# Weight decoding beside a fused attention and MLP: low parts on GpSimd, and fewer decoding steps among the early pairs

## The chip, the cores and the metric

One NeuronCore of one Trainium2 chip runs the whole program. The metric is device microseconds (us) of one execution. Five engines work beside each other, each taking its own instructions strictly in the order of its row: TensorE (PE, with its weight loads as PEld), VectorE (DVE), ScalarE (ACT), GpSimd (POOL) and SyncE (SP, which issues the transfers). [...]

## The reference

```python
def reference(q, k, v, n_global, n_local, moe_w_in, moe_w_out):   # shortened
    scores = q @ k.T / sqrt(64) - slope_h * dist      # 4 batches, 8 heads, 768 tokens, head size 64
    scores = where(is_global | is_local, scores, -1e9)   # 8 global keys, 96 local ones
    a = exp(scores - max); a = a / (sum(a) + 1e-9)
    x = (a @ v).transpose(0, 2, 1, 3).reshape(3072, 512)
    h = x @ w_in                                     # 512 x 2048
    g = h * clip(h + 3, 0, 6) / 6
    return g @ w_out                                 # 2048 x 512
```

The weights arrive as 64-bit floats. Before they can be used, each must be decoded into a high part and a low part of reduced precision, whose sum carries nearly the full 32 bits. A product of two such pairs takes three matmuls (high by high, low by high, high by low).

## The kernel before, in words

**Tiles.** The 3072 tokens are eight blocks of 384. A block has four pairs of heads (pair `n`, `n` from 0 to 31), and an MLP of sixteen slices `f` of 128 hidden units. Slice `f` takes `first` (12 matmuls, x by `w1`, into a bank `hp`), then the gate (ACT relu L185 and DVE L186 write `g`), `high` (`gh`, the rounded `g`), `rest` (`gl` = `g` - `gh`, L199), and `second` (9 matmuls with `w2` into `acc`, started by `finish`). `finish` of one slice stands on PE behind `first` of the next slice. `g` has one buffer, so the next relu waits until `gl` has been made.

**Decoding.** The weights come in 32 chunks: chunk 2f is the `w1` part of slice `f`, chunk 2f+1 its `w2` part. `decode` is a generator with four steps to a chunk: L444 and L445 on DVE clear and shift the word `wz`; the low part of the chunk *before* is made (L450); L453 puts sign and exponent in; L457 adds the last places `we`, ACT takes the magnitude of the next chunk (L410), rounds this one to its high part (L461) and makes the next `we` (L422; for the first six chunks GpSimd makes it, L415). `wz` and `we` have two buffers each; the buffer of `wz` comes free when the low part has been made, so L410 of chunk c+2 waits for the low part of chunk c.

**What sets the order.** The code is one list of instructions. `in_order` pins PE, SP and GpSimd to the order in which the code issues them. DVE and ACT are ordered by a scheduler. Decoding steps are put between the other work by a budget: `work(pe, dve)` adds to the PE time and the DVE time given out, and while the DVE sum is smaller, a decoding step is issued, whose yield is added to it. The DVE sum starts at `LEAD`. `decoded_to(i)` issues whatever is still missing of chunk `i` just before it is used: `halves` calls it for chunk 2f ahead of `first`, and `finish` for chunk 2f+1 ahead of `second`.

**Stages.** Early stage: pairs 0 to 8 are pipelined over three iterations (scores and weighing L891/L895, normalization on GpSimd L915, turning by PE transposes L923/L925, `values` L971, then `put_x` L160/L161); in the last three iterations the first three slices of block 0 stand between the turns. Common stage: 21 steps, whose block (0 or 1) is a digit of `ORDER`; the zeros are slices 3 to 15 of block 0, the ones slices 0 to 7 of block 1. Step s has `first` of its slice, the gate, and then `finish` of step s-1. After it the decoding is over; the rest of block 1 and blocks 2 to 7 follow with the remaining pairs between them.

## Time and profile before

| | |
|---|---|
| median of 3 runs | 655.08 us (653.16 to 655.09) |
| profiled execution | 654.68 us, span on the core 652.9 us |
| PE busy | 639.4 us, 98% of the span |
| DVE busy | 356.9 us, 55% |
| ACT busy | 257.4 us, 39% |
| POOL busy | 167.6 us, 26% |
| TensorE clock granted | 1.0 throughout |

The page has a line for each engine, the span in 40 slices, the DMA queues, the chain that ended last, and the costliest groups of instructions. Views of the trace give the same by window, by group (mean ns of one, and what ended the idle time before), by wait, and row by row (start us, duration us, engine, line, operation, output and inputs). A row that starts before the row above it has ended is pipelined behind it.

### The profile page before, as it was taken

What the parts mean: (1) busy time and instruction counts of PE and PEld (TensorE: products, weight loads), DVE (VectorE), ACT (ScalarE), POOL (GpSimd) and SP (SyncE); (2) the same over time, 40 slices, a digit from 0 to 9 for tenths busy, and PEclk for the clock granted to TensorE, in tenths of its full rate; (3) what the DMA queues carried; (4) which work ended last, traced back from release to release, by engine and by line L of the source; (5) the groups of instructions that cost most, each with busy time, mean ns of one, the idle gap of its engine ahead of it and who ended that gap; (6) DMA issues with size and microseconds to landing.
All of it is one profiled execution on the core that took longest, in us unless ns stands there. A gap on an engine that the chain in (4) does not pass through costs nothing.

```text
span 652.9 us, 13102 instructions
## 1 busy us (share of the span) xinstructions
PE 639.4 (98%) x4761; PEld 564.1 (86%) x4761; DVE 356.9 (55%) x1066; ACT 257.4 (39%) x706; POOL 167.6 (26%) x372
## 2 busy tenths in 40 slices
PE   8989999999999999999999999999999999999997
PEld 7778999997888889988898888888898888989985
DVE  5889999995644554255444454345542554422222
ACT  6897777775423222242313232132222423121111
POOL 5667000001422322034122332123220341202100
PEclk9999999999999999999999999999999999999999
DMA  7675644443565564346553455525643454310001
GB/s 281 182 238 194 189 157 149 143 129 113 126 189 169 147 192 125 90 118 165 164 134 102 117 154 163 141 78 154 184 126 89 122 136 122 94 43 8 1 0 54
DMA packets 47122, 86.23 MB, mean 132 GB/s; under 512 B 6504, under 2 KB 28872, under 8 KB 47048
## 3 DMA queue, kind: packets, MB, share of 16 engines
q1 hardware_dynamic: 46760, 85.03, 44.4%
q8 instruction: 40, 0.66, 0.4%
q14 instruction: 34, 0.28, 0.1%
q10 hardware_dynamic: 288, 0.26, 0.1%
HBM read 60.30 MB, written 24.97 MB: 131 GB/s over the span
## 4 chain that ended last, share of the span: by engine, by line
PE 83%; DVE 6%; ACT 4%; DMA 2%; POOL 2%; issue 2%; SPq 1%; POOLq 0%; ACTq 0%
PE hp L174 38%; PE acc L206 35%; ACT n L895 3%; PE xp L971 3%; PE sp L862 2%; PE sp L971 2%; DMA there<-blocks 1%; POOL n L915 1%; SPq L953 1%; DVE n L891 1%; PE xp L206 1%; PE tp L206 1%; PE sp L206 1%; DVE blocks L937 1%; DVE wz L453 1%
## 5 line engine op out<-in xcount | busy, mean ns | idle before, releaser
L185 ACT ACTIVATE g<-hp,small 128x384 f32<-128x384 f32 x127 | 73.6, 580 | 277.6 <-PE hp L174 173.4
L174 PE MATMUL hp<-xh,w1h 128*128 128x384 f32 x512 | 173.8, 340 | 0.5 <-ACT w1h L461 0.5
L174 PE MATMUL hp<-xh,w1l 128*128 128x384 f32 x512 | 172.3, 337 | 0.5 <-DVE w1l L450 0.5
L174 PE MATMUL hp<-xl,w1h 128*128 128x384 f32 x512 | 171.7, 335 | 0.0
L192 POOL TENSOR_SCALAR gh<-g 128x384 fp32r<-128x384 f32 x104 | 53.6, 515 | 343.6 <-DVE g L186 320.7
L186 DVE SCALAR_TENSOR_TENSOR g<-g,hp 128x384 f32<-128x384 f32 x128 | 70.7, 553 | 123.3 <-ACT g L185 122.1
L206 PE MATMUL acc<-w2h,gh 128*128 128x512 f32 x336 | 133.2, 396 | 0.0
L206 PE MATMUL acc<-w2h,gl 128*128 128x512 f32 x336 | 131.7, 392 | 0.0
L206 PE MATMUL acc<-w2l,gh 128*128 128x512 f32 x336 | 131.6, 392 | 0.0
L199 DVE TENSOR_TENSOR gl<-g,gh 128x384 fp32r<-128x384 f32 x128 | 71.5, 559 | 70.7 <-POOL gh L192 58.3
L895 ACT ACTIVATE n<-n,least 128x136 f32<-128x136 f32 (+2 forms) x192 | 79.5, 415 | 65.5 <-DVE least L891 64.8
L174 PEld LDWEIGHTS hp<-xh,w1h 128*128 128x128 f32 x512 | 96.1, 188 | 6.5 <-issue 3.1
L174 PEld LDWEIGHTS hp<-xl,w1h 128*128 128x128 f32 x512 | 96.2, 188 | 2.5
L174 PEld LDWEIGHTS hp<-xh,w1l 128*128 128x128 f32 x512 | 96.1, 188 | 1.1 <-DVE w1l L450 0.8
L915 POOL TENSOR_SCALAR n<-n,sums 128x136 f32<-128x136 f32 (+2 forms) x186 | 81.8, 457 | 38.3 <-DVE sums L906 23.1
L206 PEld LDWEIGHTS acc<-w2h,gh 128*128 128x128 f32 x336 | 63.1, 188 | 15.2 <-issue 3.3
L206 PEld LDWEIGHTS acc<-w2h,gl 128*128 128x128 f32 x336 | 63.1, 188 | 13.7 <-DVE gl L199 0.3
L206 PEld LDWEIGHTS acc<-w2l,gh 128*128 128x128 f32 x336 | 63.1, 188 | 11.4
L937 DVE STREAM_TRANSPOSE blocks<-n 128x256 f32<-128x256 f32 x138 | 51.1, 423 | 25.3 <-POOL n L915 20.8
L895 ACT ACTIVATION_READ_ACCUMULATOR n<-n,least 128x1 f32 x192 | 35.9, 187 | 0.0
L891 DVE CUSTOM_DVE_ANT_0 n<-sp,dl 128x136 f32<-128x136 f32 x60 | 17.7, 295 | 14.7 <-PE tp L862 14.7
L410 ACT ACTIVATE wz<-wst 128x512 f32<-128x512 f32 x32 | 21.5, 674 | 5.7 <-DVE w2l L450 2.8
(119 smaller groups left out, 644.6 us busy)
## 6 DMA issues: line engine op xcount, KB each, us to landing
there<-blocks SPq DMA_DIRECT2D x92, 192.0 KB
wst<-w SPq DMA_DIRECT2D x32, 512.0 KB
weights<-there SPq DMA_DIRECT2D x161, 96.0 KB
load<-pairs SPq DMA_DIRECT2D x31, 444.0 KB
load<-pairs SPq DMA_DIRECT2D x32, 384.0 KB
out<-o SPq DMA_DIRECT2D x23, 256.0 KB
weights<-there SPq DMA_DIRECT2D x23, 24.0 KB
there<-blocks SPq DMA_DIRECT2D x4, 72.0 KB
```

What stands on the lines that cost most here:

```text
L174: self.nc.tensor.matmul(hp, lhsT=self.w1(w, f)[:, kt, :], rhs=a[:, kt, :], start=(n == 0), stop=(n == 3 * NKT - 1))
L185: nc.scalar.activation(out=g, in_=hp, func=AF.Relu, bias=self.three, scale=1.0)
L186: nc.vector.scalar_tensor_tensor(out=g, in0=g, scalar=6.0, in1=hp, op0=ALU.min, op1=ALU.mult)
L192: self.nc.gpsimd.tensor_scalar(out=gh, in0=g, scalar1=1.0, scalar2=0.0, op0=ALU.mult, op1=ALU.add)
L199: self.nc.vector.tensor_tensor(out=gl, in0=g, in1=gh.bitcast(F32), op=ALU.subtract)
L206: self.nc.tensor.matmul(acc[tt], lhsT=a[:, tk], rhs=self.w2(w, f), start=(f == 0 and j == 0), stop=(f == NF - 1 and j == 2))
L410: self.nc.scalar.activation(out=self.z[i].bitcast(F32), in_=words[:, :, 1].bitcast(F32), func=AF.Abs)
L891: nc.vector.tensor_tensor_reduce(out=e[:, j, lo:end], in0=sp[j][:, lo:end], in1=d, op0=ALU.add, op1=ALU.min, scale=scale, scalar=3.0e38, a ...
L895: nc.scalar.activation(out=e[:, j, lo:end], in_=e[:, j, lo:end], func=AF.Exp, bias=self.least[:, i:i + 1], scale=-1.0, accum_out=self.sums ...
L915: nc.gpsimd.tensor_scalar(out=e[:, j, lo:end], in0=e[:, j, lo:end], scalar1=over, scalar2=0.0, op0=ALU.mult, op1=ALU.add)
L937: nc.vector.transpose(out=self.blocks[:, :, s, t].rearrange("p b j q -> p j b q"), in_=e[:, :, c:c + P].rearrange("p j (b q) -> p j b q", ...
L971: nc.tensor.matmul(xps[j * D:(j + 1) * D, t * P:(t + 1) * P], lhsT=vt[0:K, t, j * D:(j + 1) * D], rhs=self.part(t, j, c, K), start=(c == 0 ...
```

## The change

Two constants and two engine assignments change. `LEAD` goes from 6 to 14, so that the DVE budget begins higher and decoding steps come later among the early pairs. `QUIET` = 6 is new: the low part of chunk c is made by GpSimd instead of DVE for c from 6 on, and that decoding step then yields 0 to the budget. In the common stage `halves` gets `low=True`: `gl` is made by GpSimd, and the gate's second share of the DVE budget is 0 instead of 0.47. The new line numbers are one or two higher.

```diff
-LEAD = 6
+LEAD = 14
...
+QUIET = 6
...
-    def rest(self, g, gh):
+    def rest(self, g, gh, pool=False):
         gl = self.lp.tile([P, TB], F32R, name="gl")
-        self.nc.vector.tensor_tensor(out=gl, in0=g, in1=gh.bitcast(F32), op=ALU.subtract)
+        (self.nc.gpsimd if pool else self.nc.vector).tensor_tensor(out=gl, in0=g, in1=gh.bitcast(F32), op=ALU.subtract)
...
-                tt(out=lo, in0=sh(self.z.pop(i - 1).bitcast(F32)), in1=hi.bitcast(F32), op=ALU.subtract)
-            yield 0.6 * b
+                (nc.gpsimd if i > QUIET else nc.vector).tensor_tensor(out=lo, in0=sh(self.z.pop(i - 1).bitcast(F32)),
+                                                                      in1=hi.bitcast(F32), op=ALU.subtract)
+            yield 0.6 * b * (i <= QUIET)
...
-    def halves(self, steps, pool=False):
+    def halves(self, steps, pool=False, low=False):
...
-            gl = self.rest(g, gh)
-            self.work(0, 0.47)
+            gl = self.rest(g, gh, low)
+            self.work(0, 0 if low else 0.47)
...
-            for _ in self.halves(todo):
+            for _ in self.halves(todo, low=True):
```

PE has the same order before and after. Three places show what moves.

GpSimd at the start of the common stage, before: behind the masks (`dl`) stands nothing until the decoding is over, when `blocks` is cleared and the next stage's first query is scaled.

```order
L298 TENSOR_SCALAR dl_1028<-d0_85 32x128
L298 TENSOR_SCALAR dl_1028<-d1_86 32x136
L306 MEMSET blocks_1976 128x3x192
L848 TENSOR_SCALAR load0_72<-load0_72,over_1029 128x384
L192 TENSOR_SCALAR gh_2010<-g_2007 128x384
```

GpSimd at the same place, after (`gl_1056` is the gate of step 0, `gl_1109` of step 1, `gl_1138` of step 2 and so on; the low parts are those of chunks 6, then 7 and 8, 9 and 10, 11, 12).

```order
L299 TENSOR_SCALAR dl_1016<-d1_86 32x136
L200 TENSOR_TENSOR gl_1056<-g_1051,gh_1054 128x384
L451 TENSOR_TENSOR w1l0_145<-wz_1060,w1h0_144 128x4x128
L200 TENSOR_TENSOR gl_1109<-g_1104,gh_1107 128x384
L200 TENSOR_TENSOR gl_1138<-g_1133,gh_1136 128x384
L451 TENSOR_TENSOR w2l0_147<-wz_1081,w2h0_146 128x512
L451 TENSOR_TENSOR w1l0_145<-wz_1142,w1h0_144 128x4x128
L200 TENSOR_TENSOR gl_1191<-g_1186,gh_1189 128x384
L451 TENSOR_TENSOR w2l0_147<-wz_1163,w2h0_146 128x512
L451 TENSOR_TENSOR w1l0_145<-wz_1204,w1h0_144 128x4x128
L200 TENSOR_TENSOR gl_1244<-g_1239,gh_1242 128x384
L451 TENSOR_TENSOR w2l0_147<-wz_1216,w2h0_146 128x512
```

The low part of chunk 7, which `finish` of step 1 reads, now stands behind `gl` of step 2, and those of chunks 9 and 10 behind `gl` of step 3. From step 7 to step 14 two low parts stand behind each `gl`; behind the last low part, that of chunk 31, stand five `gl` alone.

DVE behind the last weighing of the early pairs, before (`wz_813` is chunk 2, `wz_848` chunk 3; chunks 0 and 1 are ready):

```order
L927 COPY pt_744<-hp_743 128x512
L905 TENSOR_SCALAR sums_706<-sums_706 128x6
L906 RECIPROCAL sums_706<-sums_706 128x6
L161 TENSOR_TENSOR xl_154<-xp_750,xh_153 128x384
L457 ISA wz_813<-wz_813,we_814 128x1024
L444 TENSOR_SCALAR wz_848<-wz_848 128x512
L445 TENSOR_SCALAR wz_848<-wz_848 128x512
L450 TENSOR_TENSOR w1l0_145<-wz_813,w1h0_144 128x4x128
L453 SCALAR_TENSOR_TENSOR wz_848<-wst_721,wz_848 128x512
L186 SCALAR_TENSOR_TENSOR g_809<-g_809,hp_796 128x384
```

DVE at the same place, after (`wz_775` and `wz_785` are chunks 0 and 1, `wz_853` is chunk 2, `wz_865` chunk 3):

```order
L929 COPY pt_724<-hp_723 128x512
L459 ISA wz_775<-wz_775,we_776 128x1024
L459 ISA wz_785<-wz_785,we_786 128x1024
L907 TENSOR_SCALAR sums_691<-sums_691 128x6
L908 RECIPROCAL sums_691<-sums_691 128x6
L451 TENSOR_TENSOR w1l0_145<-wz_775,w1h0_144 128x4x128
L162 TENSOR_TENSOR xl_154<-xp_730,xh_153 128x384
L451 TENSOR_TENSOR w2l0_147<-wz_785,w2h0_146 128x512
L187 SCALAR_TENSOR_TENSOR g_808<-g_808,hp_795 128x384
L445 TENSOR_SCALAR wz_853<-wz_853 128x512
L446 TENSOR_SCALAR wz_853<-wz_853 128x512
L200 TENSOR_TENSOR gl_849<-g_808,gh_847 128x384
```

The end of chunks 0 and 1 and all of chunk 2 have moved from among the pairs to behind them. On ACT, the magnitude of chunk 2 now stands behind the relu of the first gate, while before it stood among the early weighing:

```order
L186 ACTIVATE g_808<-hp_795,small_70 128x384
L411 ACTIVATE wz_853<-wst_779 128x512
L929 COPY pt_812<-tp_811 128x512
L195 CAST gh_847<-g_808 128x384
L411 ACTIVATE wz_865<-wst_790 128x512
```

Before, the relu of the first gate had the magnitude of chunk 3 ahead of it, that of chunk 4 behind it:

```order
L410 ACTIVATE wz_848<-wst_721 128x512
L461 CAST w1h0_144<-wz_813 128x4x128
L185 ACTIVATE g_809<-hp_796,small_70 128x384
L927 COPY pt_824<-tp_823 128x512
L410 ACTIVATE wz_911<-wst_818 128x512
```

## Prediction

> **What bounds the kernel now.** I read the engine line of the page first, then the windows, to see where PE is not busy.
>
> ```profile
> PE 639.4 (98%) x4761; PEld 564.1 (86%) x4761; DVE 356.9 (55%) x1066; ACT 257.4 (39%) x706; POOL 167.6 (26%) x372
> ```
>
> ```profile
> core 0: us, PE busy (x) PEld busy (x) DVE busy (x) ACT busy (x) POOL busy (x), PEclk, DMA share, GB/s
> 20.00:40.00 20.00, 17.88 (x191) 14.18 (x187) 17.51 (x74) 17.99 (x65) 13.10 (x27) 1.00 0.70 216
> 40.00:60.00 20.00, 17.57 (x162) 15.50 (x161) 18.64 (x51) 16.93 (x46) 15.19 (x32) 1.00 0.62 203
> 120.00:140.00 20.00, 20.00 (x101) 18.03 (x101) 18.98 (x39) 15.32 (x27) 0.00 (x0) 1.00 0.50 157
> 140.00:160.00 20.00, 19.04 (x137) 16.36 (x137) 14.28 (x32) 11.80 (x22) 2.65 (x4) 1.00 0.27 75
> ```
>
> In the common stage (60 to 150 us) PE is busy all of the time although DVE is at 95%: DVE is full, but nobody waits for it. GpSimd does nothing there. What could be won on PE is in the early stage (2.1 and 2.4 us idle in the two windows) and at the end of the decoding (1.0 us). The waits of PE and its rows say which:
>
> ```profile
> PE tp L923 <- ACT pt L927: 1.0, 1, 1.0
> PE hp L174 <- DVE w1l L450: 0.5, 1, 0.5
> PE hp L174 <- ACT w1h L461: 0.5, 1, 0.5
> ```
>
> ```profile
> 28.44 1.32 PE L971 MATMUL xp<-pt,load 128*64 128x128 f32 x20 [0.55 <-DVE xl L161]
> 32.98 1.32 PE L971 MATMUL xp<-pt,load 128*64 128x128 f32 x20 [0.24 <-DVE xl L161]
> 38.53 1.54 PE L971 MATMUL xp<-pt,load 128*64 128x128 f32 x24 [1.05 <-DVE xl L161]
> 44.31 1.54 PE L971 MATMUL xp<-pt,load 128*64 128x128 f32 x24 [1.42 <-issue]
> 46.63 0.42 PE L174 MATMUL hp<-xh,w1h 128*128 128x384 f32 x1
> 51.21 0.43 PE L174 MATMUL hp<-xh,w1h 128*128 128x384 f32 x1
> ```
>
> Successive `values` rows are one iteration of the pairs. Without decoding on DVE one takes 4.54 us (28.44 to 32.98), with it 5.55 and 5.78. The last two rows are `first` of slices 0 and 1. In the chain, the last `values` of the early stage and what follows:
>
> ```profile
> 63.58 1.25 PE xp L971 x20
> 64.82 2.28 PE hp L174 x12
> 73.34 2.10 PE hp L174 x12
> 75.45 2.08 PE acc L206 x9
> ```
>
> A common step takes PE 2.10 + 2.08 = 4.18 us. The prices of single instructions, from the groups by form:
>
> ```profile
> L185 ACT ACTIVATE g<-hp,small 128x384 f32<-128x384 f32 x127 | 73.6, 580 | 277.6 <-PE hp L174 173.4 <-DVE gl L199 96.3 <-DVE blocks L937 3.2
> L199 DVE TENSOR_TENSOR gl<-g,gh 128x384 fp32r<-128x384 f32 x128 | 71.5, 559 | 70.7 <-POOL gh L192 58.3 <-PE acc L206 12.1 <-POOL load L848 0.3
> L186 DVE SCALAR_TENSOR_TENSOR g<-g,hp 128x384 f32<-128x384 f32 x128 | 70.7, 553 | 123.3 <-ACT g L185 122.1
> L192 POOL TENSOR_SCALAR gh<-g 128x384 fp32r<-128x384 f32 x104 | 53.6, 515 | 343.6 <-DVE g L186 320.7 <-PE acc L206 16.5 <-ACT xh L160 4.0
> L457 DVE CUSTOM_DVE_ANT_0 wz<-wz,we 128x1024 uint16<-128x1024 uint16 x32 | 22.7, 710 | 1.6 <-POOL we L415 0.9
> L453 DVE SCALAR_TENSOR_TENSOR wz<-wst,wz 128x512 int32<-128x512 int32 x32 | 22.5, 704 | 0.0
> L410 ACT ACTIVATE wz<-wst 128x512 f32<-128x512 f32 x32 | 21.5, 674 | 5.7 <-DVE w2l L450 2.8 <-DVE w1l L450 2.3
> L422 ACT ACTIVATE we<-wst 128x512 int32<-128x512 uint32 x26 | 17.5, 674 | 0.0
> L445 DVE TENSOR_SCALAR wz<-wz 128x512 int32<-128x512 int32 x32 | 13.8, 432 | 0.3
> L444 DVE TENSOR_SCALAR wz<-wz 128x512 f32<-128x512 f32 x32 | 13.7, 429 | 0.2 <-ACT wz L410 0.2
> L194 ACT CAST gh<-g 128x384 fp32r<-128x384 f32 x24 | 12.3, 511 | 3.3 <-DVE g L186 2.9
> L450 DVE TENSOR_TENSOR w1l<-wz,w1h 128x512 fp32r<-128x512 f32 x16 | 11.1, 694 | 0.0
> L461 ACT CAST w1h<-wz 128x512 fp32r<-128x512 f32 x16 | 9.9, 621 | 1.7 <-DVE wz L457 1.0
> ```
>
> **The price of the new GpSimd instructions.** No row has a two-input operation of this size there. One-input rows, and DVE beside GpSimd:
>
> ```profile
> 30.78 0.69 POOL L415 TENSOR_SCALAR we<-wst 128x512 int32<-128x512 uint32 x1
> 44.50 2.64 POOL L915 TENSOR_SCALAR n<-n,sums 128x232 f32<-128x232 f32 x6 [3.21 <-DVE least L891]
> 47.22 1.93 POOL L415 TENSOR_SCALAR we<-wst 128x512 int32<-128x512 uint32 x2
> ```
>
> ```profile
> 54.26 1.14 DVE L453 SCALAR_TENSOR_TENSOR wz<-wst,wz 128x512 int32<-128x512 int32 x1
> 55.93 1.15 DVE L457 CUSTOM_DVE_ANT_0 wz<-wz,we 128x1024 uint16<-128x1024 uint16 x1
> ```
>
> Lower ends: what one input costs there, 0.69 us for 128x512 and 0.52 for 128x384. Upper ends: twice that, if the inputs are read one after the other, 1.38 and 1.04. On DVE the second input makes 0.69 (L450) of 0.43 (L444), a factor of 1.6; I take the same here: 1.10 for a low part, 0.83 for `gl`. [...] No run so far shows such an instruction.
>
> **What is taken off DVE** is worth nothing by itself: 26 low parts (18.0 us) and 21 `gl` (11.7 us) lie in a stage where PE waited only at its end. Its last 1.0 us, the two waits of 0.5, goes: -1.0, or 0 if the decoding is late again.
>
> **What costs nothing.** On SP three loads of chunks move behind loads of pairs; the transfers' share of 0.62 in the window from 40 leaves room, and each chunk is loaded two chunks ahead. On GpSimd `blocks` and the next stage's first query now stand behind the last `gl`, some 3.7 us behind the stage's last `first` (2.5 and the two rows' 0.58 and 0.59). Before, the query was scaled at 151.55 and first used in a matmul near 158:
>
> ```profile
> 150.87 0.58 POOL L306 MEMSET blocks<- 128x576 f32 x1 [88.63 <-DVE wz L453]
> 151.55 0.59 POOL L848 TENSOR_SCALAR load<-load,over 128x384 f32<-128x384 f32 x1
> ```
>
> ```profile
> 158.40 1.01 PE acc L862 x47
> ```
>
> So over 2 us of cover stay; if it went, the cost would be what of the 3.7 us stands out, under 2.
>
> **Less decoding among the pairs (term A).** Out of DVE's row between the pairs go two L457, two L450, and L444, L445, L453 of chunk 2: 1.42 + 1.39 + 1.57 = 4.4 us. Two iterations fall from 5.55 and 5.78 to about 4.55 and 4.6, so the pairs are 2.2 us early: the `values` at 44.31 comes at 42.1. But all that work now stands between PE and its first slices. Pair 7 is normalized by 44.2 (2.64 us), then GpSimd makes two `we` (0.69 each, 45.6), DVE two L457 (0.6 more behind the second: 46.4), the sums of pair 8 (0.3) and `w1l` of chunk 0 (0.7, 47.5). The third matmul of `first` 0 needs that, and ten of its twelve follow in 1.8: it ends at 49.3, before at 48.8. Chunk 2 starts behind this gate's relu: relu 0.58, magnitude 0.67, L444 0.43, L445 0.43, `gl` 0.56, L453 0.70, chunk 3's L444 0.43, an `xl` of about `gl`'s size 0.56, L457 0.71, chunk 3's L445 and L453 1.13 (which cover the 0.62 of the high part), `w1l` 0.69. That is 6.9, and 6.4 with overlaps of some 0.05 to 0.08 between neighbours: 55.7. `first` 1 ends at 57.6; it began at 51.21 before and ended near 53.4. PE then has 9.0 us to the last `values` (three turns, `values`, two `second`, `first` 2): 66.6, say 66.7, against 63.58, where before lost 1.0 behind ACT (the wait for `pt` above) that falls away. A = +3.1. It is +1 if chunk 3 and `xl` don't stand in the way, and +5 if two DVE rows stretch as those at 54.26 and 55.93 did, and the `we` as at 47.22.
>
> **GpSimd's fixed row (term B).** A low part waits for the `gl` ahead of it, this one for a gate, that for `first`: relu, L186, L194, `gl`, 0.58 + 0.55 + 0.51 + 0.83 = 2.5 us behind the end of `first`. Between `first` of step s and that of s+1 PE has 2.08 us of work; the first use of a `w1` low part is the third matmul (0.35 us in), that of a `w2` low part the second (0.23 us). Step 0 starts at 67.9 (66.7 and `values` 1.25).
> - Chunk 6 (behind `gl` of step 0, used by `first` of step 1): `first` ends 70.0, `g` 71.35, `gh` behind an L422 72.3, `gl` 73.15, low part 74.25; PE is there at 72.4. +1.85.
> - Chunk 7 (behind `gl` of step 2, used by `finish` of step 1, right behind `first` of step 2): `first` ends 80.4, `g` 81.75, `gh` 82.3, `gl` 83.15, low part 84.25; PE is there at 80.65. +3.6.
> - Chunk 10. The buffers of chunks 9 and 10 come free with the low parts of 7 and 8, at 84.25 and 85.35. From 85.4 on: magnitude 86.05, then DVE with both chunks' rows in turn to 88.5, `we` 88.75, L457 89.5, high part 90.1, next `we` 90.7, and only then the relu of step 3 on ACT, 91.2; gate and `gl` 93.2, low parts 94.3 and 95.4. PE wants it at 90.65. +4.75.
> - Chunk 11 by the same chain behind `gl` of step 4: 103.25 against 101.75, +1.5. Chunk 12 behind `gl` of step 5: 107.6 against 105.45, +2.15.
>
> B = 13.85. With the lower prices the five are 1.15, 2.9, 3.65, 1.15 and 1.35, 10.2 in all; the upper ones give about 16.5. The waits of ACT's L410 for L450 in its group row (2.8 and 2.3) show that the two buffers of `wz` do hold it up.
>
> **The dense steps (term C).** From step 9 to 14 two chunks are decoded per step, in two buffers; each goes round once per step: 0.67 + 0.43 + 0.43 + 0.70 + 0.71 + 0.62 + 1.10 = 4.66, with seven hand-overs of some 0.03 (L415 ends at 31.47, L457 starts at 31.50) 4.9, and 5.0 with something of a gate on DVE between. PE needs 4.18: +0.8 for six steps, C = +4.9. The lower price gives +1.8, the upper one +7.
>
> **Sum**, against the profiled execution: 654.68 + 3.1 + 13.85 + 4.9 - 1.0 = 675.5 us. That execution lies inside the three timed runs, 0.06% under their median, 655.08. From the lower ends it is 654.68 + 1 + 10.2 + 1.8 - 1 = 666.7, from the upper 654.68 + 5 + 16.5 + 7 = 683.2.
>
> **Rivals.**
> *PE stays the bound.* Were the low part of chunk 7 done within 0.23 us of the end of `first` of step 2, GpSimd's row would cost nothing; the pairs' gain of 2.2 and the waits of 1.0 and 1.0 would come through, 654.68 - 4.2 = 650.5, or 653 with half of it. For it speaks that GpSimd is idle in the whole stage; against it that the gate's four instructions alone take 2.5 us, and that the order of that row is fixed. 0.09. Something between that and no change: 0.04.
> *Only the first two waits.* PE, once late, might find the later low parts ready: 654.68 + 3.1 + 1.85 + 3.6 - 1.0 = 662.2. Against it: the buffers tie chunks 9 and 10 to the late low parts, so lateness is passed on. 0.12.
> *DVE stretched beside GpSimd.* L453 and L457 took 1.14 and 1.15 beside L415, 0.44 more than their means. If both do so for both chunks of the six dense steps, 4 x 0.44 x 6 = 10.6 more: 686. For it: those two rows. Against it: most low parts come while DVE waits. 0.07. [...]
>
> **Chances.** Forecast 0.68, first two waits 0.12, stretched 0.07, faster 0.09, between 0.04. The range 661 to 687 takes in the first three but for a little at its ends. About 0.3% (2 us, the spread of the three runs) is what a measurement can tell from no change: faster 0.09, same 0.04, slower 0.87.
>
> **What the profile after would show.** PE's list of waits led by GpSimd's low parts: L451 ahead of L175 and L207, single waits of 3 us and more, all before 115 us; PE well under 20 in the windows from 60 to 120; GpSimd busy 45 us (26 x 1.10 + 21 x 0.83) between 65 and 170; the `values` now at 44.31 about 2 us earlier, `first` 1 some 4 us later; common steps of about 5 us between steps 9 and 14, then 4.18 again. I am wrong if PE is busy throughout the common stage: then either a low part is much shorter than 0.69 or the row is not kept as written. If single waits are there but the later ones are missing, the second rival holds.

## The result, and the profile after

The kernel after takes 707.31 us (median of 4 runs, 704.65 to 707.71), the kernel before 654.88 (653.16 to 655.09): a ratio of 1.0798, 95% interval 1.0766 to 1.0831. The direction was forecast, the size was not: 675.5 us, at most 687. Four executions that ran far longer than the others of their kernel (702 to 2245 us) are left out of all comparisons, which leaves two for the kernel with a third buffer, below, and no interval.

The engine line of the page, and PE's list of waits (engine, line, what it waited for: us in all, times, longest):

```profile
PE 656.9 (93%) x4761; PEld 574.3 (82%) x4761; DVE 358.8 (51%) x1019; ACT 258.7 (37%) x706; POOL 224.0 (32%) x419
```

```profile
PE acc L207 <- POOL gl L200: 9.5, 4, 2.7
PE hp L175 <- POOL w1l L451: 9.2, 4, 3.0
PE sp L207 <- POOL gl L200: 6.3, 3, 2.9
PE acc L207 <- POOL w2l L451: 4.3, 2, 3.9
```

DVE's busy time is larger than before (358.8 against 356.9), although 47 of its instructions, 29.7 us, have gone to GpSimd. The groups by form say where it went:

```profile
L455 DVE SCALAR_TENSOR_TENSOR wz<-wst,wz 128x512 int32<-128x512 int32 x32 | 34.2, 1067 | 0.8
L459 DVE CUSTOM_DVE_ANT_0 wz<-wz,we 128x1024 uint16<-128x1024 uint16 x32 | 29.9, 933 | 3.3 <-POOL we L416 1.3 <-ACT we L423 0.6
L200 POOL TENSOR_TENSOR gl<-g,gh 128x384 fp32r<-128x384 f32 x21 | 24.4, 1160 | 52.0 <-issue 31.0 <-ACT gh L195 17.7 <-PE xp L207 3.2
L451 POOL TENSOR_TENSOR w1l<-wz,w1h 128x512 fp32r<-128x512 f32 x13 | 17.7, 1359 | 15.6 <-ACT w1h L463 15.6
L445 DVE TENSOR_SCALAR wz<-wz 128x512 f32<-128x512 f32 x32 | 15.3, 478 | 20.7 <-ACT wz L411 20.7
```

L455 and L459 (L453 and L457 before) do what they did, in 1067 and 933 ns in place of 704 and 710: 18.8 us more for 32 chunks. And DVE stood idle 20.7 us ahead of L445, waiting for the next magnitude (L411), which itself waited 17.2 us for low parts of GpSimd to give up a `wz`. The windows (columns as before: PE, PEld, DVE, ACT, POOL busy, granted clock) show two different stretches. First one of the kernel before, then the kernel after:

```profile
80.00:100.00 20.00, 20.00 (x103) 18.24 (x102) 19.26 (x40) 15.56 (x28) 0.00 (x0) 1.00 0.49 148
```

```profile
80.00:100.00 20.00, 13.75 (x53) 11.48 (x52) 7.08 (x13) 8.71 (x15) 7.29 (x7) 0.83 0.25 79
100.00:120.00 20.00, 16.03 (x62) 14.11 (x63) 12.81 (x22) 10.27 (x19) 7.05 (x7) 0.83 0.33 104
140.00:160.00 20.00, 15.39 (x62) 12.70 (x60) 19.09 (x26) 12.18 (x21) 9.96 (x7) 0.86 0.46 137
160.00:180.00 20.00, 12.60 (x50) 9.98 (x50) 19.21 (x24) 12.22 (x22) 11.28 (x9) 0.90 0.38 127
```

From 80 to 100 PE, DVE, ACT and GpSimd all wait: PE is busy 13.75 us in place of 20.00, DVE only 7.08 in place of 19.26. From 140 to 180 DVE is full and PE waits for it.

To see where the time is lost I take the relu of a common step's gate as a clock: step 0, 9, 16 and 20 (of 0 to 20). In the kernel before the fourth of these rows starts at 152.26 us and the first three are

```profile
67.14 0.58 ACT L185 ACTIVATE g<-hp,small 128x384 f32<-128x384 f32 x1 [0.24 <-PE hp L174]
104.70 0.58 ACT L185 ACTIVATE g<-hp,small 128x384 f32<-128x384 f32 x1 [1.16 <-PE hp L174]
...
133.96 0.58 ACT L185 ACTIVATE g<-hp,small 128x384 f32<-128x384 f32 x1 [0.94 <-DVE wz L457]
```

In the kernel after the fourth starts at 202.32 us and the first three are

```profile
72.95 0.58 ACT L186 ACTIVATE g<-hp,small 128x384 f32<-128x384 f32 x1 [0.99 <-PE hp L175]
132.04 0.58 ACT L186 ACTIVATE g<-hp,small 128x384 f32<-128x384 f32 x1 [1.46 <-PE hp L175]
...
186.76 0.58 ACT L186 ACTIVATE g<-hp,small 128x384 f32<-128x384 f32 x1
```

The lateness is 5.8, 27.3, 52.8 and 50.1 us: 5.8 before step 0 (term A: 3.1 forecast), 21.5 up to step 9 (term B: 13.85), 25.5 from step 9 to 16 (term C: 4.9), and 2.7 won back at the end of the decoding (1.0 forecast). The end of the span is 50.0 us late too (702.9 against 652.9), so nothing is lost or won behind the decoding. (The profiled executions are 50.0 us apart, the medians 52.4.)

### The profile page after: what moved, and what is told of

Read it like the earlier page. It is cut to its first block, busy times and chain, and to the rows that moved or that the text cites. A ratio compares the mean times of both kernels' runs of the same rounds, so it can differ in the third digit from the quotient of the medians.

```text
span 702.9 us, 13105 instructions
## 1 busy us (share of the span) xinstructions
PE 656.9 (93%) x4761; PEld 574.3 (82%) x4761; DVE 358.8 (51%) x1019; ACT 258.7 (37%) x706; POOL 224.0 (32%) x419
## 4 chain that ended last, share of the span: by engine, by line
PE 68%; DVE 7%; POOL 2%; DMA 2%; issue 2%; ACT 1%; SPq 1%; DVEq 0%; POOLq 0%; ACTq 0%
PE hp L175 31%; PE acc L207 30%; DVE wz L455 2%; PE sp L864 2%; PE xp L973 2%; PE sp L973 2%; DVE wz L459 2%; DMA there<-blocks 1%; SPq L955 1%; DVE wz L446 1%; POOL w2l L451 1%; DVE wz L445 1%; ACT n L897 1%; DVE blocks L939 1%; POOL w1l L451 1%
## 5 line engine op out<-in xcount | busy, mean ns | idle before, releaser
L175 PE MATMUL hp<-xh,w1l 128*128 128x384 f32 x512 | 175.7, 343 | 10.5 <-POOL w1l L451 9.2
L175 PE MATMUL hp<-xh,w1h 128*128 128x384 f32 x512 | 177.1, 346 | 4.2 <-ACT w1h L463 4.2
L175 PE MATMUL hp<-xl,w1h 128*128 128x384 f32 x512 | 174.7, 341 | 0.0
L187 DVE SCALAR_TENSOR_TENSOR g<-g,hp 128x384 f32<-128x384 f32 x128 | 70.7, 552 | 146.2 <-ACT g L186 145.2
L207 PE MATMUL acc<-w2h,gl 128*128 128x512 f32 x336 | 134.4, 400 | 9.5 <-POOL gl L200 9.5
L175 PEld LDWEIGHTS hp<-xh,w1l 128*128 128x128 f32 x512 | 98.6, 192 | 12.4 <-POOL w1l L451 10.5
L175 PEld LDWEIGHTS hp<-xh,w1h 128*128 128x128 f32 x512 | 98.8, 193 | 10.9 <-ACT w1h L463 5.1
L200 DVE TENSOR_TENSOR gl<-g,gh 128x384 fp32r<-128x384 f32 x107 | 59.7, 558 | 70.2 <-POOL gh L193 58.2
L917 POOL TENSOR_SCALAR n<-n,sums 128x136 f32<-128x136 f32 (+2 forms) x186 | 79.2, 444 | 39.6 <-DVE sums L908 25.5
L200 POOL TENSOR_TENSOR gl<-g,gh 128x384 fp32r<-128x384 f32 x21 | 24.4, 1160 | 52.0 <-issue 31.0
L455 DVE SCALAR_TENSOR_TENSOR wz<-wst,wz 128x512 int32<-128x512 int32 x32 | 34.2, 1067 | 0.8
```

The source lines that it names most:

```text
L175: self.nc.tensor.matmul(hp, lhsT=self.w1(w, f)[:, kt, :], rhs=a[:, kt, :], start=(n == 0), stop=(n == 3 * NKT - 1))
L187: nc.vector.scalar_tensor_tensor(out=g, in0=g, scalar=6.0, in1=hp, op0=ALU.min, op1=ALU.mult)
L200: (self.nc.gpsimd if pool else self.nc.vector).tensor_tensor(out=gl, in0=g, in1=gh.bitcast(F32), op=ALU.subtract)
L207: self.nc.tensor.matmul(acc[tt], lhsT=a[:, tk], rhs=self.w2(w, f), start=(f == 0 and j == 0), stop=(f == NF - 1 and j == 2))
L455: stt(out=z, in0=self.raw[i].rearrange("p (c w) -> p c w", w=2)[:, :, 1], scalar=-0x40000000, in1=z, op0=ALU.bitwise_and, op1=ALU.bitwise_or)
L917: nc.gpsimd.tensor_scalar(out=e[:, j, lo:end], in0=e[:, j, lo:end], scalar1=over, scalar2=0.0, op0=ALU.mult, op1=ALU.add)
```

## Experiments

Differences are to the kernel before on the same chip in the same comparison; the last three columns are the lateness gained in the three parts of the trace, read from the relu rows as above. What is gained or won back behind step 16 is not in them.

| kernel | us | against before | ratio (95%) | to step 0 | 0 to 9 | 9 to 16 |
|---|---|---|---|---|---|---|
| after | 707.3 | +52.4 | 1.0798 (1.0766 to 1.0831) | 5.8 | 21.5 | 25.5 |
| LEAD 14 alone | 663.0 | +7.7 | 1.0121 (1.0103 to 1.0139) | 6.9 | 1.2 | 0.8 |
| after, all on DVE again | 662.5 | +7.3 | 1.0113 (1.0091 to 1.0135) | 5.9 | 1.3 | 0.8 |
| `gl` alone | 660.0 | +4.8 | 1.0073 (1.0054 to 1.0093) | -0.1 | 4.2 | 2.7 |
| low parts alone | 679.4 | +24.1 | 1.0378 (1.0351 to 1.0404) | 2.2 | 13.9 | 10.6 |
| both, LEAD and budget of before | 698.1 | +43.2 | 1.0659 (1.0631 to 1.0688) | 1.1 | 21.0 | 9.7 |
| after, LEAD 6 | 694.5 | +39.6 | 1.0599 (1.0572 to 1.0625) | 0.7 | 23.0 | 16.6 |
| after, row not fixed | 685.6 | +30.7 | 1.0468 (1.0440 to 1.0496) | 7.2 | 13.2 | 8.6 |
| same, LEAD 6 | 681.7 | +26.8 | 1.0413 (1.0389 to 1.0438) | 2.2 | 13.5 | 10.3 |
| low parts in quarters | 676.4 | +21.5 | 1.0318 (1.0289 to 1.0346) | 2.4 | 8.5 | 7.3 |
| same, third `wz` | 684.9 | +29.6 | 1.0461 (1.0422 to 1.0500) | 1.8 | 18.8 | 8.3 |
| low parts of one input | 661.5 | +6.2 | 1.0097 (1.0065 to 1.0128) | 1.4 | 3.9 | 2.8 |
| after, all of one input | 680.6 | +25.8 | 1.0403 (1.0373 to 1.0433) | 5.4 | 12.9 | 5.6 |
| after, idle matmuls in waits | 705.9 | +50.6 | 1.0758 (1.0713 to 1.0802) | 7.7 | 21.0 | 24.7 |
| after, third `wz` | 703.3, 705.6 | +48, +50 | none | 5.6 | 22.2 | 20.2 |
| LEAD 9 alone | 660.6 | +5.7 | 1.0087 (1.0072 to 1.0102) | 3.6 | 1.2 | 0.7 |
| last three low parts | 655.3 | +0.4 | 1.0017 (0.9998 to 1.0035) | 0.5 | 0.0 | 0.0 |

### Which part costs what

**LEAD alone.** `-LEAD = 6` / `+LEAD = 14` in the kernel before.

> The kernel before with LEAD at 14 and nothing else: only less of the decoding among the early pairs; all low parts and gl stay on VectorE. My theory (the lateness of the stage's start is a cost by itself, 5.7 us in the trace after: `values` 8 at 69.3 against 63.6): 654.9 + 4 to 6 = 659 to 661, and part of it may grow, since VectorE is full up to the end of the decoding and has 4.4 us more to do there: up to 665. Rival (the lateness comes only with GpSimd's row, or is made good by the common stage's slack): 654 to 656.

662.96: 7.7 more, above my 4 to 6 but inside what I allowed for DVE. PE's rows that waited, around slices 0 and 1 of this kernel:

```profile
48.12 0.69 PE L174 MATMUL hp<-xh,w1l 128*128 128x384 f32 x1 [0.84 <-DVE w1l L450]
57.18 0.46 PE L174 MATMUL hp<-xh,w1h 128*128 128x384 f32 x1 [1.84 <-ACT w1h L461]
```

Slice 1 starts 6 us later than before (51.21), as slice 0's weights are late and chunk 2 stands behind its gate. The lateness is made here (6.9 us at step 0) and is not won back (8.1 at step 20).

**The close packing without GpSimd.** The kernel after, with L451 and L200 given back to `nc.vector`; LEAD and the yields stay.

> The kernel after with its LEAD and its budgets (the decoding as closely packed as there), but the low parts and gl made by VectorE again. My theory (the cost is what GpSimd's instructions do, as waits in its fixed row and as stretching of VectorE, and the clock that follows): most of the 52.4 us go, 660 to 670, what is left being the later start and a VectorE that is late in the close steps. Rival (the close packing of the decoding makes the long steps, whoever does the low parts): 690 to 707, with steps of 7 us and more between 140 and 180.

662.53, as LEAD alone. But the close packing did not stay. DVE's rows show it, when the last instruction of each chunk (L459 in the kernel after, L458 here) is counted between the gates: from step 9 to step 16 the kernel after finishes two chunks in every step, 14 in all, this kernel and the kernel before nine. In every step of the stage this kernel finishes as many as LEAD alone. So the changed budget costs nothing while the work stays on DVE, and 45 of the 52 us come only when the 47 instructions go to GpSimd; whether by what they do or by the closer row on DVE that the scheduler then makes, this run can't say.

**`gl` alone**, and **low parts alone**, each in the kernel before with its LEAD and its budget:

```diff
...
-            for _ in self.halves(todo):            # gl alone
+            for _ in self.halves(todo, low=True):
...
-                tt(out=lo, ...)                    # low parts alone
+                (nc.gpsimd if i > QUIET else nc.vector).tensor_tensor(out=lo, ...)
```

> The kernel before with only the common slices' gl on GpSimd; low parts on VectorE, budgets and LEAD as before. My theory (the waits come from low parts that stand behind a gl in GpSimd's row; gl alone has a whole step until it is used): PE waits for a gl seldom, VectorE is relieved by 0.56 us a step but stretched by some 0.5 us while a gl runs: 653 to 659. Rival (every instruction on GpSimd beside VectorE costs by stretching): 21 x 0.5 to 1.0 us = 10 to 20 more, 665 to 675.

> The kernel before with only the low parts from the seventh chunk on on GpSimd; gl on VectorE, budgets and LEAD as before. My theory of the fixed row (a low part waits because a gl stands ahead of it): these waits go, since nothing stands in GpSimd's row but low parts; what stays is 0.67 us more per chunk in the round of the two wz buffers (some 4.9 us for two chunks against 5.2 that they come apart), and stretched L453 and L457: 656 to 668. Rival (the stretching alone makes the long steps: about 1.6 us for each of 26 chunks on a VectorE that is full): 680 to 700.

`gl` alone came out between the two, near mine. The low parts alone decided against me: 679.4, where the fixed row should have cost nothing, since no `gl` stands in it. PE now waits for the gates that DVE makes (14.7 us), not for a low part: every step from 0 to 16 takes 4.6 to 6.8 us in place of 4.2. The groups of this kernel, and four rows of GpSimd and DVE in order of time:

```profile
L455 DVE SCALAR_TENSOR_TENSOR wz<-wst,wz 128x512 int32<-128x512 int32 x32 | 39.8, 1245 | 0.9
L446 DVE TENSOR_SCALAR wz<-wz 128x512 int32<-128x512 int32 x32 | 22.1, 692 | 0.7
```

```profile
103.21 1.28 POOL L451 TENSOR_TENSOR w1l<-wz,w1h 128x512 fp32r<-128x512 f32 x1 [2.36 <-ACT w1h L463]
103.31 1.73 DVE L455 SCALAR_TENSOR_TENSOR wz<-wst,wz 128x512 int32<-128x512 int32 x1
...
106.60 1.30 POOL L451 TENSOR_TENSOR w2l<-wz,w2h 128x512 fp32r<-128x512 f32 x1 [2.11 <-ACT w2h L463]
106.70 1.48 DVE L446 TENSOR_SCALAR wz<-wz 128x512 int32<-128x512 int32 x1
```

GpSimd begins at 103.21 and ends at 104.49; DVE's L455 begins 0.10 behind it and ends at 105.04, 0.55 behind its end. The row reads as if it stood still until GpSimd is through, and then took most of its usual 0.70. L446, with one input, the same (ends 0.28 behind). It is so each time: between 64 and 190 us, 17 of L455 and 8 of L446 start behind a low part in this way, and all of them end 0.54 to 0.56 and 0.28 to 0.29 us behind its end. Over the kernel L455 grew by 0.54 us and L446 by 0.26, 25.6 us for 32 chunks; DVE was spared 26 low parts, 18.0 us. **GpSimd took more of DVE's time than the work it took over.** For `gl` the same sum is 13.0 (L457 897 ns, L445 652 ns) against 11.7 spared. Not all of the 24.1 has to be this: DVE's row is closer than before as well, and finishes its last chunk behind the gate of step 15 in place of step 19.

**Both, with LEAD and budget of before; and the kernel after with LEAD 6.**

> The kernel before with both groups on GpSimd (low parts from the seventh chunk on, gl of the common slices), LEAD and budgets as before. If the two groups add up: 655.3 + 4.8 + 24.1 = 684. My theory (a low part stands behind a gl in the fixed row, and both hold up VectorE): more than the sum, 686 to 697, with waits of PE for low parts that neither group alone had. If it comes out as the kernel with LEAD 6 of this group does, within 2 us, the packing of the decoding is without a part in it.

> The kernel after with LEAD back at 6; all else of the change stays. The earlier runs gave LEAD alone +7.7 us and LEAD with the packing +7.3. If the parts add up: 707.3 - 7.5 = 699.8, between 697 and 702. Rival (the later start also makes the waits in GpSimd's row, because less is decoded ahead when the first gl comes): 680 to 693.

698.1 and 694.5. Both groups together cost 43.2, 14.3 more than their sum. The row explains it, in which low parts now stand behind `gl` (PE waits 17.7 us for `w1l`, which neither group alone had); a further 10.4 us of its lateness come between steps 16 and 20. LEAD in the kernel after is worth 12.8 and not 7.7, so some 5 us come only where the late start and GpSimd's row meet; both of my alternatives (697 to 702, or 680 to 693) missed. The closer budget even gains 3.6.

### How GpSimd holds DVE

**Quarters.** Low parts alone on GpSimd, each as four instructions of 128 columns.

```diff
...
+                    for q in range(4):
+                        c = q if i % 2 else slice(q * P, (q + 1) * P)
+                        nc.gpsimd.tensor_tensor(out=lo[:, c], in0=zl[:, c], in1=hi[:, c].bitcast(F32), op=ALU.subtract)
```

> The kernel before with only the low parts from the seventh chunk on on GpSimd, each as four instructions of 128 columns in place of one of 512. In the trace of the unsplit one VectorE's L455 began 0.1 us behind a low part and ended 0.55 us behind its end. My theory (whichever of the two engines has begun holds the other for that whole instruction): a quarter holds it for 0.35 us at most, so L455 falls from a mean of 1.25 to 0.8 to 1.0 us, L446 from 0.69 to about 0.5, and the time from 679.4 to 660 to 670; the quarters in their turn wait for VectorE. Rival (the two share a rate while both run): L455 and L446 stretch as before, four starts cost more than one, 679 to 690.

```profile
L455 POOL TENSOR_TENSOR w1l<-wz,w1h 128x128 fp32r<-128x128 f32 x52 | 38.7, 774 | 19.8 <-ACT w1h L468 19.8
L460 DVE SCALAR_TENSOR_TENSOR wz<-wst,wz 128x512 int32<-128x512 int32 x32 | 26.2, 818 | 0.9
L411 ACT ACTIVATE wz<-wst 128x512 f32<-128x512 f32 x32 | 21.3, 669 | 39.0 <-POOL w2l L455 19.0 <-POOL w1l L455 16.9 <-DVE w2l L457 1.6
L464 DVE CUSTOM_DVE_ANT_0 wz<-wz,we 128x1024 uint16<-128x1024 uint16 x32 | 27.8, 870 | 1.5 <-POOL we L416 0.9
```

The groups of this kernel say that the mechanism is as I said, but not that the hold is gone: L446 is back at 434 ns, L460 (L455 above) falls from 1245 to 818, while L464 (L459 above) rises from 709 to 870 and DVE's own `gl` from 558 to 599. Against the kernel before, these three are longer by 13.9 us in all, where low parts in one piece cost 25.6. If the two engines shared a rate, cutting the instruction up would not have helped DVE. But the time fell by some 3 us only, and neither range held it. Much of what DVE no longer waits, GpSimd does: a quarter takes 0.75 us on average (0.45 at the shortest), a low part three us, and ACT's magnitude waits 36 us for it to give up a `wz`.

**Quarters with a third `wz`.** `bufs + (bufs > 1)` for the pool `zp`.

> The kernel with the low parts in quarters on GpSimd (676.4) with a third wz buffer. In its trace VectorE is hardly held any more (L446 0.43, L460 0.82), but a low part takes 4 x 0.75 us, and ScalarE's next magnitude waited 36 us for GpSimd to give a buffer back. My theory (what is left of that kernel's cost is the round of two buffers): 658 to 668. Rival (the two engines still pass the same time between them, and it shows up elsewhere): 673 to 678.

684.9, some 8 us *slower* than with two, against both expectations. ACT's waits for GpSimd fell to 22 us, but DVE is full again (19.73 and 19.25 of 20 in the windows from 60 and 80, against 17.85 and 15.73) and PE waits for gates that stand behind the decoding (17.5 us for DVE's `gl` and ACT's `gh`). DVE finishes two chunks in each of the steps 2 to 11. So the decoding, let run ahead, makes the gates late; that the two engines pass the same time between them fits, but isn't shown by itself.

**One input.** Low parts alone, made from `hi` alone (times 2^-12; so 26 chunks have other low parts).

> The kernel before with the low parts from the seventh chunk on on GpSimd, but made from the high part alone (times 2^-12): one input in place of two, so the low parts of 26 chunks are other numbers. It starts where the low part of two inputs starts (behind the high part), and gives the wz buffer back earlier. My theory (GpSimd holds VectorE for as long as its instruction lasts, whatever it reads): 0.69 us in place of 1.36, so L455 falls from a mean of 1.25 us to 0.8 to 0.95 and L446 from 0.69 to about 0.5; 658 to 668. Rival (only two inputs on GpSimd get in VectorE's way): L455 at 0.70, L446 at 0.43, and VectorE is simply relieved of 18 us: 652 to 656.

```profile
L458 DVE SCALAR_TENSOR_TENSOR wz<-wst,wz 128x512 int32<-128x512 int32 x32 | 28.5, 891 | 0.9
L446 DVE TENSOR_SCALAR wz<-wz 128x512 int32<-128x512 int32 x32 | 16.4, 512 | 0.4
L453 POOL TENSOR_SCALAR w1l<-w1h 128x512 fp32r<-128x512 f32 x13 | 9.5, 730 | 31.7 <-ACT w1h L466 31.7
```

661.5, as I expected: an instruction of half the length (0.73 against 1.38), with one input, still holds DVE, for 8.5 us in all (0.19 and 0.08 on the mean of 32) against 25.6. The rows say by what: 18 of L458 and 7 of L446 start behind a low part and end 0.52 to 0.55 and 0.27 to 0.29 us behind its end, just as with two inputs. So the hold lasts as long as GpSimd's instruction does. And in every step DVE finishes as many chunks as with low parts alone, so the 17.9 us between the two kernels are not the packing; the hold differs by 17.1. That it still costs 6.2, though DVE is spared 18, I can explain only in part: DVE has 19.4 of 20 us busy up to 140 and is nearly through then, the first fifteen steps take 4.4 to 4.8 us, and PE waits 3.6 us for DVE's `gl`. The scheduler has put the decoding closer than in the kernel before (the last chunk ends behind the gate of step 15, not 19) and gates behind it; what that alone costs is open, as no run kept DVE's row as it was.

**All of one input, in the kernel after** (26 low parts from `wz` and 21 `gl` from `gh` alone, times 2^-12; GpSimd's order and the buffers as in the kernel after).

> The kernel after with its 26 low parts and 21 gl on GpSimd made from one input each (wz or gh times 2^-12), so both are other numbers; order, waits and buffers as in the kernel after, but 0.70 and 0.52 us in place of 1.36 and 1.16. If the time is set by how long an instruction of GpSimd lasts (it holds VectorE for that long, and the row of gate, gl and low parts is longer by it): the long steps fall from 7.6 to some 5.5 us (7 x 2.1 = 15) and five waits by 1.0 to 1.3 us: 684 to 690. If it is the order of the row alone (gate, gl, low part, then the next magnitude), whose other links take 3 us and more: 697 to 703.

680.6, even below the range of the first. With GpSimd's row as it was, shorter instructions take 26.7 of the 52.4 us away: 8.6 between steps 0 and 9 and 19.9 between 9 and 16. Two other things moved a little: a low part made from `wz` alone no longer waits for the rounding of the high part (0.62 us on ACT), and DVE finishes 12 chunks between steps 9 and 16 in place of 14. Over the kernel L460 and L464 are back at

```profile
L460 DVE SCALAR_TENSOR_TENSOR wz<-wst,wz 128x512 int32<-128x512 int32 x32 | 24.0, 749 | 0.7
L464 DVE CUSTOM_DVE_ANT_0 wz<-wz,we 128x1024 uint16<-128x1024 uint16 x32 | 22.9, 716 | 4.7 <-POOL we L419 1.3 <-ACT we L426 1.3
```

### The row, the buffers and the clock

**The row not fixed**, with LEAD 14 and with LEAD 6: `in_order` passes over GpSimd's `gl` and low parts, so that the scheduler sets low parts ahead of the `gl` of the same step (the first two rows are chunk 6, then `gl` of step 0).

```diff
...
+                if i.name in self.free:      # names of these 47 instructions
+                    continue
```

> The kernel after, but its gl and low parts on GpSimd are not tied into the fixed order of that engine's instructions: the scheduler puts the low part of a chunk ahead of the gl of the step where its model has it ready first. My theory (the row's waits of 12.9 us and the lower clock behind them come from the order): 707.3 - 13 to 18 = 689 to 694, with the long steps of 7 us still there. Rival (the low parts are late because VectorE and the two buffers hold up the decoding, whatever the row): 702 to 708.

> The kernel after with LEAD at 6 and with gl and low parts not tied into GpSimd's fixed order. The two alone took 12.8 and 21.7 us off. If they take away different costs: 707 - 34 = 673, which is less than the low parts alone cost (679). If both take away the same waits in part (my theory: the row's waits, which a late start makes worse): 678 to 688, what is left being VectorE held by GpSimd, 24 us for the low parts and some for gl.

685.6 and 681.7. Freeing the row takes 21.7 off, more than I gave it, and then LEAD is worth only 3.9. (DVE's row gets looser with it, 10 chunks between steps 9 and 16 in place of 14, so the 21.7 are not GpSimd's order alone.) What is left with LEAD 6, 26.8, is about what the two groups cost when each is alone (28.9). With LEAD 14 the long waits for low parts are gone from PE's list (two, 1.6 us); what remains is waiting for `gl` and `gh`, 15.8 us.

**A third `wz` in the kernel after.**

> The kernel after with a third wz buffer in the early stage and the common one, nothing else. My theory of term B (the late low parts hold both buffers, so VectorE waits for the next magnitude: 20.7 us of its idle time stand behind L411): most of these waits shrink, the waits of chunks 10 to 12 go or halve, 690 to 699. Rival (the order of GpSimd's row and the holding of one engine by the other set the time, the buffers only follow): 703 to 708.

703.3 and 705.6: the rival. The waits for low parts keep their size (13.8 us against 13.5 in PE's list). Steps 9 to 16 gain 5.3 us, of which half is lost again behind step 16. The two buffers mostly pass lateness on; they make little of it.

**Idle matmuls in the waits.** Behind the wait at 88.34 in the kernel after PE runs at about half its rate: `first`'s matmuls come every 0.32 us, later every 0.17 (rows of PE; granted clock 0.53 from 90 to 94.5, 1.00 from 94.5 to 96).

```profile
93.52 0.52 PE L175 MATMUL hp<-xh,w1l 128*128 128x384 f32 x1
93.84 0.52 PE L175 MATMUL hp<-xh,w1h 128*128 128x384 f32 x1
...
94.55 0.33 PE L175 MATMUL hp<-xh,w1h 128*128 128x384 f32 x1
94.72 0.34 PE L175 MATMUL hp<-xl,w1h 128*128 128x384 f32 x1
```

The next kernel keeps PE busy there: `bank[:, TB:BANK]` gets 8, 9 and 9 matmuls ahead of `first` of slices 3, 5 and 6 of block 0, and 12 ahead of `second` of slice 3. Two of its windows follow the expectation.

> The kernel after with idle matmuls on PE in four of the five long waits for a low part: 8 or 9 of 128x128 into unused columns of the bank ahead of the first of slices 3, 5 and 6 of the first block, 12 ahead of the second of slice 3. All else as in the kernel after. My theory (after a wait of 3 to 4 us PE runs at a granted clock of about 0.6 for 3 to 6 us, which costs by itself): the windows from 90 and from 100 us come back to 1.0, and 4 to 6 us go: 701 to 704. Rival (PE is waiting for the decoding anyway, so a faster PE only waits longer): 706 to 709, the low clock gone all the same.

```profile
80.00:100.00 20.00, 17.59 (x105) 15.84 (x105) 8.31 (x15) 8.58 (x16) 7.00 (x7) 1.00 0.28 84
100.00:120.00 20.00, 17.16 (x85) 15.24 (x86) 13.59 (x22) 10.10 (x19) 7.41 (x7) 0.91 0.30 89
```

The granted clock from 80 to 100 is back at 1.00 (0.83 in the kernel after) and 0.91 from 100 to 120 (0.83). The time is that of the kernel after within both intervals, and steps 0 to 9 cost 21.0 in place of 21.5. The higher clock gained at most these 0.5 us. In these nine steps the low clock is a mark of the waits, not a cost beside them; in the later steps it was not tried.

### Is there anything to win?

**LEAD 9**, and **the last three low parts** (`QUIET = 29`), each alone in the kernel before.

> The kernel before with LEAD at 9, all else as before: one chunk less is decoded among the early pairs, in place of three. With 14 the pairs came 1.0 and 2.1 us earlier but slice 0 waited 1.5 us and slice 1 came 6 us later. My theory: with one chunk less slice 0 has its weights in time and a pair is 0.5 to 1 us early, but slice 1's chunks are later by one too: 653.5 to 658. Rival (each chunk less costs its share of the 7.7): 657 to 659.

> The kernel before with only the last three low parts (chunks 29 to 31) on GpSimd. There PE waits for the decoding's end, 0.5 us twice, and the stage after it has little on VectorE. My theory: the ends cancel, since a low part is 0.7 us longer there and holds one L453 or L457: 654 to 657. Rival (VectorE free 2 us earlier at the end takes the waits away): 653.5 to 654.3, the only part of the change that could win.

660.6: one chunk less among the pairs already costs 5.7, more than either expectation. The `values` at 44.31 comes 0.4 us early (43.88), but slice 1 waits for chunk 2:

```profile
55.02 0.45 PE L174 MATMUL hp<-xh,w1h 128*128 128x384 f32 x1 [2.97 <-ACT w1h L461]
```

The last three low parts can't be told from no change. No run points to a version faster than the kernel before.

## Why the prediction was wrong

**What bounds the kernel** was read rightly: PE is the bound, DVE is full and nobody waits for it, GpSimd idle. The conclusion that 29.7 us off DVE are worth nothing by themselves was too kind: I took it that they at least leave DVE. They did not: L455 and L459 alone grew by 18.8 us, and DVE's busy time rose.

**The price of a GpSimd instruction.** Taken at 1.10 and 0.83; at the shortest it is 1.26 and 0.99, on average 1.36 and 1.16, so the upper ends (1.38, 1.04) were the ones to take. With them in terms B and C the sum would have been 675.5 + 2.65 + 2.1 = 680.3: this was not the error that mattered. (GpSimd is busy 59.8 us with the 47 instructions; the forecast said 45, though its own terms add up to 46.)

**Term A, 3.1** (ends 1 and 5). 5.8 in the trace, 7.7 as a run of its own. The chain was right in kind: `values` now at 42.32 (42.1 forecast), slice 0 waits for its low part, slice 1 is late. But the high part of chunk 2 came at 55.98 where I had its low part at 55.7, and PE ran the rest of slice 1 at a low clock (0.32 us a matmul; granted 0.59 from 56 to 60). With LEAD 9 the same wait is there.

**Term B, 13.85.** The five single waits are there, at the places named:

```profile
77.98 0.45 PE L175 MATMUL hp<-xh,w1l 128*128 128x384 f32 x1 [2.63 <-POOL w1l L451]
88.34 0.79 PE L207 MATMUL acc<-w2l,gh 128*128 128x512 f32 x1 [3.92 <-POOL w2l L451]
100.67 0.44 PE L175 MATMUL hp<-xh,w1l 128*128 128x384 f32 x1 [3.00 <-POOL w1l L451]
109.07 0.50 PE L207 MATMUL acc<-w2l,gh 128*128 128x512 f32 x1 [0.43 <-POOL w2l L451]
114.41 0.45 PE L175 MATMUL hp<-xh,w1l 128*128 128x384 f32 x1 [2.87 <-POOL w1l L451]
```

12.85 us, against 1.85, 3.6, 4.75, 1.5 and 2.15. The mechanism (gate, `gl`, low part, then the next magnitude) stands, and freeing the row took nearly all of these waits away. That their sum is so near the forecast is luck in part: single ones are off by up to 1.75, both ways. And the nine steps lost 21.5. The windows of 5 us between 75 and 130 have PE idle for 13.8 us, hardly more than those waits; most of the rest is work at a low clock, 0.74, 0.58, 0.66 and 0.69 in four of them (5 x 1.33 = 6.7 us), the lowest being

```profile
90.00:95.00 5.00, 5.00 (x17) 4.52 (x17) 3.61 (x7) 2.52 (x5) 0.00 (x0) 0.58 0.43 132
```

I had no term for that. The idle matmuls showed that it is not to be added: with the clock back, the nine steps still took 21.0 more. What the rest of the 21.5 is, no run separates; the low parts alone, without any `gl` in the row, lose 13.9 there.

**Term C, 4.9, is the step that failed.** I had a step of two chunks at 5.0 us, from the round of two buffers, with DVE's instructions in it at their old prices of 0.70 and 0.71. It takes 7.6. PE's list of waits is led by `gl` (15.8 us), not by the low parts as forecast (13.5), and these waits stand in the long steps. One such step, GpSimd and DVE, then PE:

```profile
156.53 1.30 POOL L451 TENSOR_TENSOR w2l<-wz,w2h 128x512 fp32r<-128x512 f32 x1 [1.28 <-ACT w2h L463]
156.63 1.74 DVE L455 SCALAR_TENSOR_TENSOR wz<-wst,wz 128x512 int32<-128x512 int32 x1
158.30 0.54 DVE L187 SCALAR_TENSOR_TENSOR g<-g,hp 128x384 f32<-128x384 f32 x1
160.18 1.27 POOL L451 TENSOR_TENSOR w1l<-wz,w1h 128x512 fp32r<-128x512 f32 x1 [2.35 <-ACT w1h L463]
160.27 1.72 DVE L455 SCALAR_TENSOR_TENSOR wz<-wst,wz 128x512 int32<-128x512 int32 x1
161.40 1.45 POOL L200 TENSOR_TENSOR gl<-g,gh 128x384 fp32r<-128x384 f32 x1
162.13 1.27 DVE L459 CUSTOM_DVE_ANT_0 wz<-wz,we 128x1024 uint16<-128x1024 uint16 x1
```

```profile
162.90 0.80 PE L207 MATMUL acc<-w2h,gl 128*128 128x512 f32 x1 [2.73 <-POOL gl L200]
```

A low part holds L455 (1.74, 1.72), which keeps the gate's L187 back; `gl` stands behind the next low part and in turn holds L459. Between 143 and 186 us L455 takes 1.72 and L459 1.05 on average: 2 x (0.42 + 0.43 + 1.72 + 1.05) + 0.54 = 7.8, less some overlap: DVE's row, not the buffers (with a third buffer these seven steps still lose 20.2). Seven steps like it, one of them of 10.3, are the 25.5; with the short instructions they lose 5.6. (The lower end of this term, +1.8, comes to some 2.4 by its own figures; that changes nothing.)

**The rival "DVE stretched"** named this and had 0.07. It was mis-sized twice: by 0.44 us an instruction from the two rows beside a one-input L415 of 0.69, where the new instructions are twice as long, and only for the dense steps, where the low parts alone cost 13.9 before step 9 too. "Most low parts come while DVE waits" was the wrong argument against it: DVE is full. Those two rows already had the same delay in them: L415 ran from 54.20 to 54.86 and from 55.54 to 56.54, and L453 and L457 ended at 55.40 and 57.08, both 0.54 behind it. The row at 103.31, with two inputs, ended 0.55 behind its low part, L446 at 106.70, with one, 0.28; what in the hardware holds them, no run shows. As an estimate from these rows, with lengths from the trace, every new instruction can hold DVE for its whole length, 26 x 1.36 + 21 x 1.16 = 59.7 us at most against 29.7 spared; put in place of term C, that gives 675.5 - 4.9 + 30.0 = 700.6.

**The others.** "PE stays the bound" fell at once. "Only the first two waits" fell: all five came. What was forecast to cost nothing (transfers, the next stage's query) cost nothing behind step 20. Loads of chunks did turn up among the waits (ACT 1.4 us, GpSimd 5.3, early). The same waits of 1.4 and 5.3 stand in the kernel with all on DVE again, so they are no part of what GpSimd costs; whether they cost anything by themselves was not tried.

**The whole, 52.4**, from the runs: 7.7 for LEAD, 24.1 for the low parts and 4.8 for `gl`, and some 16 that appear only together (fixed row, 14.3 with LEAD 6, a little more with 14). Of the 24.1, 17.9 go when GpSimd's instruction is half as long at equal packing, and are the hold on DVE as far as the rows show (it falls by 17.1, and PE waits for no low part in either kernel). The other 6.2, what is left of the hold and the closer row on DVE, are not separated. The split between row and hold is not sharp either: shortening the instructions shortens the row too (-26.7), and freeing the row alone gives -21.7.

## What to carry to other kernels

Before work goes from a full DVE to an idle GpSimd, add each GpSimd instruction's length to DVE's row and not only to GpSimd's: here, with the low parts alone, each took 0.69 us off DVE and put 0.98 on. An engine that nobody waits for but that is full (DVE before, 18.80 to 19.93 of 20 us in the windows from 60 to 140) is a cover that is nearly gone, so a change that adds to it must be counted in full. And an idle engine whose row is fixed turned, here, a producer that was late by one gate into a late decoder (five waits of PE for low parts, 12.85 us).

## What was not expected of the hardware

- A DVE instruction of the decoding with two inputs that started while GpSimd made a low part or `gl` in one piece ended 0.52 to 0.56 us behind GpSimd's end, whether that took 1.28 us with two inputs (L455 at 103.31 with the low parts alone, 1.73 in place of 0.70) or 0.72 on average with one (L458, 0.89 on the mean of 32); one with one input ended 0.27 to 0.29 behind it (L446 at 106.70, 1.48 in place of 0.43). L187, whose inputs are the bank `hp` and one tile, was not held in the one row that started so: in the kernel after it took 0.56 at 187.37, wholly beside a low part that ran from 186.93 to 188.23.
- Cut into quarters, GpSimd's 128x512 took 3.0 us beside a busy DVE (a quarter 0.75 on average, 0.45 at the shortest), against 1.38 in one piece.
- Behind waits of PE of 2.48, 2.87, 3.00 and 3.92 us (ending at 139.04, 114.41, 100.67 and 88.34 in the kernel after) the granted clock was 0.50 to 0.56 over the next 3 us; behind the one of 2.63 us (77.98) it stayed at 1.00. So the length of the wait alone did not decide it here.
